# Row turns of the first expert slot placed one per two attention stages; an overflow loop over 128-row chunks; the first dense block's rows turned before that loop

## The chip, the cores and the metric

The kernel runs on one core of one Trainium2 chip. The metric is the device time of one execution in microseconds (us); the median of three runs of the kernel before is 809.47 us (807.54 to 810.33). PE is the matrix engine, DVE, ACT and POOL the vector, scalar and general engines, SP the engine that issues most DMAs.

## The reference

Three layers in float32, cut to what matters:

```
x = attention(q, k, v)             # 4 batches, 8 heads, 576 positions, 64 wide, window 128, slope bias
x = x.transpose(0,2,1,3).reshape(2304, 512)
logits = x @ w_gate + modality_bias[modality_id]      # 8 experts
e = argmax(logits); g = softmax(logits)[e]
y[rows of e] = g * (relu(x[rows of e] @ w1[e]) @ w2[e])   # 512 -> 1024 -> 512
out = relu(y @ w_in)**2 @ w_out                           # 512 -> 2048 -> 512
```

Which rows go to which expert is known only on the chip, so the number of work slots is too.

## The kernel before

**Attention** runs over 40 units (batch, 128-row tile, half of the heads), in software-pipelined stages k = 0 to 42. Stage k takes the row maximum of unit k on DVE (`smax`, L243, or L245 for the 64-row tail tiles), its exponentials on ACT (`sexp`, L264/L266, in two halves), the scores of unit k+1 on PE (L228/L230), the transposes of unit k-2 (L287) with their evictions on ACT (`ev`, L298), and the product with v of unit k-3 (L322). After every second unit a generator `post` copies a tile (L342), turns it back with the router's weights beside it (L351), scales it (L353, L354, L366, L367) and stores it to `xd`. `route` then finds, three tiles at a time, each row's expert and place (L395 to L438).

The program order is written out by hand: each engine executes its instructions in the order in which the source issues them. `background()` advances every open generator by one step; a stage calls it twice, before and after `pv`.

**The first slot** (512 rows of one expert among the first 1024 tokens) is prepared during attention by the generator `prefetch_first`: it reads the slot's row list, gathers four blocks of 128 rows (L637), loads the first weight chunks, and *turns* each block. `turn` transposes 128 x 512 on PE into a bank `v` (the bank that `tr` uses too), casts the two halves on ACT (L650) and subtracts on DVE (L652), which gives a high and a low float32r part. `wsplit` does the same for a weight chunk: the high part by a cast (L567; for the first three chunks on DVE, `quick`), the low part by a subtraction (L568; on POOL, but for the first chunk on DVE). From stage 40 the generator `up_first` puts the slot's first matrix products (L657) between the rest of attention.

**Expert slots.** Five slots are unrolled. Each is 96 matmuls up, 24 per 128 rows down, and a scatter of rows to `yd` (L693). The last 128 rows of slot 4 are held back (`ylast`): their part for the first 256 output rows is added by a 0/1 matrix (`hot`).

**The loop** (L963) does further slots of 512 rows where the routing needs them. In this execution it is not entered. Every engine branches over its body all the same, and then waits until all engines and DMAs are done.

**The dense layer** works on nine blocks of 256 rows. For block 0, after the loop, `yload(0)` loads two row tiles from `yd` (L995), four matmuls with `hot` give the held-back part (L657 into `v`), DVE adds it (L1008), and `turn` makes the split transposes (L645 into `x` and `m`, L650, L652). Then `up` and `down` follow for all blocks.

Of the kernel before, what the change touches and what calls it, by code (L numbers as in the profile page):

```python
# [20 lines left out]
E, FF = 8, 1024  # L21
# [27 lines left out]
def attention_moe_kernel(ctx, tc, qh, kh, v, mid, wg, mb, w1, w2, win, wout, out):  # L49
# [22 lines left out]
    def row(dt=F32):  # L72
        return take(("row", dt), 8, lambda: rowp.tile([128, DM], dt, tag="row", name="row"))

# [15 lines left out]
    e_int, o_int = x_int[:, 0, :], x_int[:, 1, :]  # L90
    n_int = ct([1, 1], "n_int", I32)
    again = ct([128, 1], "again")
    lbias = ct([128, NT, E], "lbias")
# [380 lines left out]
    def slots():  # L474
# [36 lines left out]

        left, oh, sw, mn, need = r1([MAXSLOT]), r1([MAXSLOT]), r1([2]), r1([1]), r1([1])
        n = ends[:, E - 1:E]
# [10 lines left out]
        dve.tensor_copy(cum[0:1, 0, :], need.to_broadcast([1, E]))  # L524
        dve.tensor_tensor(n_int, n, need, op=ALU.add)
        dve.scalar_tensor_tensor(oh[:, 1:], left[:, 1:], mn, siota[:, 1:], op0=ALU.is_le, op1=ALU.mult)
# [18 lines left out]
        dve.tensor_tensor(x, x, x2, op=ALU.add)  # L545
        dve.tensor_copy(x_int[:, :, 1:MAXSLOT], x[:, :, 1:])

    second = []
# [72 lines left out]

    def index(s, o):
        iv = sm.tile([128, 4], I32, tag="idx", name="idx", bufs=3)
        if s == 0:
            pool.tensor_copy(iv, t_first[:, bass.ds(o, 4)])
            gv = sm.tile([128, 4], I32, tag="idx", name="idx", bufs=3)
            pool.tensor_scalar(gv, iv, float(DUMP), None, op0=ALU.min)
        else:
            pool.tensor_copy(iv, t_int[:, bass.ds(o, 4)])
            gv = iv  # L630
        xr[s] = iv, {}, gv
# [7 lines left out]
    def turn(s, i, r, tag, n=512):  # L639
        if s not in xT:  # L640
            k = min(4, 1024 // n)
            xT[s] = [[wt("right", F32R)[:, :k * n].rearrange("p (c t) -> p c t", t=n) for _ in range(4 // k)] for _ in range(2)]
        p = bank(tag, (128, 4, 128))
# [10 lines left out]
    def passes(ps, pairs, first, last):  # L654
        n = len(pairs)
        for i, (l, r) in enumerate(pairs):
            pe.matmul(ps, l, r, start=first and i == 0, stop=last and i == n - 1)  # L657

# [89 lines left out]
    def prefetch_first():  # L748
        index(0, column(0))
        advance_load(2)  # L750
        yield
        for i in range(0, 4):
            gather(0, i)
            yield
        advance_split(1)
        advance_load(3)
        yield
        for i in range(4):
            turn(0, i, xr[0][1][i], "v")
            yield  # L760
            if i % 2:
                advance_split(2 + i // 2)
        primed.append(True)

    primed = []
    LA = 5
# [41 lines left out]
    for k in range(n + 3):  # L808
# [31 lines left out]
    wpools["left"] = ctx.enter_context(tc.tile_pool(name="wl", bufs=24))  # L840
    assert checked
    while not primed:
        background()
# [10 lines left out]
    def down_first(hs):  # L854
# [30 lines left out]
        advance_split(8 + LA)  # L885

    while not up:
        next(first, None)
        background()

    for s in range(NSLOT):
# [21 lines left out]
        if s == 2:  # L913
            p = bank("v", (128, E))
            pe.matmul(p, ones, cum[:, 0, :], start=True, stop=True)
            dve.tensor_scalar(again, p[:, 0:1], float(ROWS), None, op0=ALU.mult)
            total = nc.values_load(n_int[0:1, 0:1], min_val=NSLOT - 1, max_val=MAXSLOT)
        if s == 0:
            down_first(hs)
            continue  # L920
        for i in range(n // 128):
# [29 lines left out]
    conv_step(2 * len(MOE_CHUNKS) + 1)  # L951
    flush(0)


# [7 lines left out]
    held.append({})  # L962
    with tc.For_i(NSLOT - 1, total, 1) as si:  # L963
        e = nc.sync.value_load(e_int[0:1, bass.ds(si, 1)], min_val=0, max_val=E - 1)
        o = pool.value_load(o_int[0:1, bass.ds(si, 1)], min_val=0, max_val=E * NCH - 4)
        index("d", o)
        for i in range(4):
            gather("d", i)
            turn("d", i, xr["d"][1][i], "x")
        hs = []  # L970
        for f in range(8):
            if f % 2 == 0:
                wload("d", expert_src(e, f // 2))
                wsplit("d")
            hs.append(relu_split(ffn1("d", W["d"], f)))
        ps = [bank("t"), bank("t"), bank("v"), bank("v")]
        for f in range(8):
            if f % 2 == 0:
                wload("d", expert_src(e, 4 + f // 2))
                wsplit("d")  # L980
            for i in range(4):
                c = slice(128 * i, 128 * i + 128)
                ffn2(ps[i], hs[f][0][:, c], hs[f][1][:, c], W["d"], f, f == 0, f == 7)
        for i in range(4):
            put("d", i, ps[i])
    held.clear()

    yr = {}

    def yload(j):  # L990
        yr[j] = []
        for i in range(2):
            r = row()
            a = row_of(2 * j + i)
            nc.sync.dma_start(out=r, in_=yd[a:a + 128, :])  # L995
            yr[j].append(r)

    order = token_tiles()
    NB = NT // 2


    yload(0)
    s, i, y, yhl, hot = ylast
    dve.tensor_tensor(yhl[:, 512:], y, yhl[:, :512].bitcast(F32), op=ALU.subtract)
    yadd = [bank("v") for _ in range(2)]
    for j in range(2):
        passes(yadd[j], [(hot[:, 128 * j:128 * j + 128], yhl[:, 512 * k:512 * k + 512]) for k in range(2)], True, True)
        dve.tensor_tensor(yr[0][j], yr[0][j], yadd[j], op=ALU.add)  # L1008
    scatter(s, i, y)
    del ylast, y, yhl, hot, yadd, xr[s]  # L1010
    for i in range(2):
        turn(("c", 0), i, yr[0][i], "xm"[i], 256)
    flush(0)
# [156 lines left out]
```

## Time and profile before

| what | us |
|---|---|
| median of three runs | 809.47 |
| the profiled execution's own time | 807.53 |
| its span, first to last instruction | 805.8 |
| PE busy in the span | 780.5 (97%) |
| DVE, ACT, POOL busy | 407.2, 330.9, 232.9 |
| attention until the first slot's products start | 0 to 147.3 |
| five expert slots (with the end of attention) | 147.3 to 375.1 |
| from the last slot product to the first dense product | 375.1 to 385.5 |
| dense layer | 385.5 to 801.9 |

Times are us from the span's start unless a row says ns. A timeline row gives start, duration, engine, line, operation, output and input tiles, and in brackets how long the engine stood idle before it and what ended that.

### The profile page before, as it was taken

The numbers are of one execution on the slowest core, as the hardware profiler recorded it, in microseconds if no ns is written. First come the engines' busy times: TensorE is split into PE (matmuls) and PEld (weight loads), VectorE is DVE, ScalarE is ACT, GpSimd is POOL, SyncE is SP. The second block draws the span as 40 slices with busy tenths as digits, with TensorE's granted clock in tenths as the row PEclk, the third lists the DMA queues.
The fourth block names the chain that finished last, engine by engine and source line by source line (L and its number), as shares of the span: only waits on it lengthen the run. The fifth ranks groups of instructions, "written<-read, shape, count | busy, mean of one in ns | idle before, by whom it ended". The sixth has DMA issues, their size and how long they took to land.

```text
span 805.8 us, 13572 instructions
## 1 busy us (share of the span) xinstructions
PE 780.5 (97%) x4979; PEld 669.2 (83%) x4979; DVE 407.2 (51%) x1134; ACT 330.9 (41%) x890; POOL 232.9 (29%) x302
## 2 busy tenths in 40 slices
PE   6999989999999999997999999999999999999998
PEld 5877767777888888895988989898998989898896
DVE  5888788879996668695464522031212213021220
ACT  7787767335454444462543414031231404132230
POOL 3010032134544434423343505032230504122140
PEclk9999999999999999999899999999999999999999
DMA  8456360149746566351110210010101001010000
GB/s 274 158 179 192 119 197 27 67 141 357 251 165 205 187 208 209 132 197 55 40 53 27 80 53 27 1 53 1 53 1 31 22 1 53 1 53 1 27 1 27
DMA packets 39190, 79.10 MB, mean 98 GB/s; under 512 B 6608, under 2 KB 15056, under 8 KB 39120
## 3 DMA queue, kind: packets, MB, share of 16 engines
q1 hardware_dynamic: 36080, 68.23, 25.5%
q0 software_dynamic: 3040, 9.96, 3.4%
q8 instruction: 41, 0.67, 0.3%
q14 instruction: 29, 0.24, 0.1%
HBM read 62.19 MB, written 15.99 MB: 97 GB/s over the span
## 4 chain that ended last, share of the span: by engine, by line
PE 52%; DMA 0%; ACT 0%; DVE 0%; issue 0%; SPq 0%; DVEq 0%
PE t L657 20%; PE v L657 16%; PE s L657 13%; PE x L657 1%; PE m L657 1%; PE x L645 1%; PE m L645 0%; DMA row<-yd 0%; ACT w L567 0%; DVE row L1046 0%; ACT w L650 0%; DVE w L568 0%; DVE w L652 0%; DVE row L1031 0%; ACT row L1030 0%
## 5 line engine op out<-in xcount | busy, mean ns | idle before, releaser
L657 PE MATMUL t<-w,h 128*128 128x512 f32 x888 | 214.4, 397 | 0.0
L657 PEld LDWEIGHTS t<-w,h 128*128 128x128 f32 x888 | 164.4, 188 | 37.8
L1021 POOL TENSOR_TENSOR h<-row,h 128x256 fp32r<-128x256 f32 x144 | 109.5, 764 | 272.1 <-ACT h L1020 266.7
L657 PE MATMUL s<-w 128*128 128x256 f32 (+2 forms) x1176 | 181.4, 310 | 1.1 <-ACT w L650 0.7
L657 PEld LDWEIGHTS s<-w 128*128 128x128 f32 x1176 | 162.9, 191 | 12.3 <-ACT w L650 1.1
L657 PE MATMUL v<-w,h 128*128 128x512 f32 x432 | 104.7, 396 | 0.0
L657 PEld LDWEIGHTS v<-w,h 128*128 128x128 f32 x432 | 80.2, 188 | 18.7
L264 ACT ACTIVATE e<-x,m 128x256 f32<-128x256 f32 (+1 forms) x128 | 60.6, 476 | 27.8 <-DVE m L243 27.6
L568 DVE TENSOR_TENSOR w<-w 128x1024 fp32r<-128x1024 f32 x42 | 57.5, 1373 | 18.8 <-ACT w L567 18.4
L1031 DVE SCALAR_TENSOR_TENSOR row<-s,row 128x256 f32<-128x256 f32 x74 | 31.3, 423 | 70.5 <-ACT row L1030 70.3
L1020 ACT CAST h<-row 128x256 fp32r<-128x256 f32 x144 | 57.7, 400 | 5.0 <-DVE row L1031 5.0
L652 DVE TENSOR_TENSOR w<-x,w 128x512 fp32r<-128x512 f32 (+1 forms) x13 | 7.7, 605 | 90.4 <-ACT w L650 90.4
L1030 ACT ACTIVATE row<-s 128x256 f32<-128x256 f32 x74 | 28.3, 384 | 55.6 <-PE s L657 54.7
L567 ACT CAST w<-w 128x1024 fp32r<-128x1024 f32 x46 | 48.0, 1048 | 6.6 <-PE s L657 2.6
L657 PE MATMUL t<-w 128*128 128x256 f32 x384 | 48.3, 282 | 0.0
L603 POOL TENSOR_TENSOR w<-w,row 128x512 int32<-128x512 int32 x18 | 26.9, 1492 | 72.8 <-DVE row L602 41.2
L657 PEld LDWEIGHTS t<-w 128*128 128x128 f32 x384 | 47.2, 190 | 0.3
L650 ACT CAST w<-x 128x512 fp32r<-128x512 f32 (+1 forms) x13 | 6.6, 521 | 98.3 <-PE x L645 96.5
L228 PE MATMUL s<-kS,qS 64*128 64x256 f32 (+1 forms) x128 | 35.8, 406 | 5.4 <-DMA qS<-qh 5.2
L657 PE MATMUL v<-w 128*128 128x256 f32 x288 | 36.2, 282 | 0.0
L228 PE MATMUL t<-kS,qS 64*128 64x256 f32 (+1 forms) x128 | 35.9, 407 | 0.0
L657 PEld LDWEIGHTS v<-w 128*128 128x128 f32 x288 | 35.4, 190 | 0.3
(242 smaller groups left out, 1064.7 us busy)
## 6 DMA issues: line engine op xcount, KB each, us to landing
w<-w SPq DMA_DIRECT2D x40, 512.0 KB, 4.3
w<-win SPq DMA_DIRECT2D x16, 512.0 KB, 5.3
w<-wout SPq DMA_DIRECT2D x16, 512.0 KB, 3.9
xd<-row SPq DMA_DIRECT2D x22, 256.0 KB, 2.1
qS<-qh SPq DMA_DIRECT2D x19, 256.0 KB, 4.4
row<-yd SPq DMA_DIRECT2D x18, 256.0 KB, 2.6
vS<-vh SPq DMA_DIRECT2D x16, 256.0 KB, 4.1
out_dram<-row SPq DMA_DIRECT2D x16, 256.0 KB, 2.0
```

What stands on the lines that cost most here:

```text
L228: pe.matmul(s[j][:, i, c0:], qS[b, t][r, hp, :], kS[b][r, hp, 128 * t - 128 + c0:128 * t + 128], start=True, stop=True)
L264: act.activation(e[:, i, j, c0:], x[:, i, j, c0:], AF.Exp, bias=m[:, i, j:j + 1], scale=-1.0, accum_out=rinv[b, t][:, h:h + 1])
L567: (dve.tensor_copy if quick else act.copy)(h, r)
L568: (eng or dve).tensor_tensor(l, r, h.bitcast(F32), op=ALU.subtract)
L603: pool.tensor_tensor(a, a, r, op=ALU.add)
L645: pe.transpose(p[:, c, :], r[:, 128 * c:128 * c + 128], ident)
L652: dve.tensor_tensor(xl[j][:, :, o], p[:, k * j:k * j + k, :], xh[j][:, :, o].bitcast(F32), op=ALU.subtract)
L657: pe.matmul(ps, l, r, start=first and i == 0, stop=last and i == n - 1)
L1020: act.copy(g[:, 0:256], gt)
L1021: pool.tensor_tensor(g[:, 256:512], gt, g[:, 0:256].bitcast(F32), op=ALU.subtract)
L1030: act.activation(r, p, AF.Relu)
L1031: dve.scalar_tensor_tensor(gt, p, 0.0, r, op0=ALU.max, op1=ALU.mult)
```

## The change

Four edits. (1) `prefetch_first` turns its four row blocks at the second `background()` of stages 33, 35, 37 and 39 (a flag `tail` tells it the stage), where before it took one step at each call from stage 32 on; the low part of the first weight chunk is made on POOL. (2) The loop's body works on one chunk of 128 rows in place of four; its bounds and its tables (`loop_int`) count chunks. (3) The loads of the first dense block's rows are issued after the slot's second tile is scattered; `turn_first` turns these rows by float32 matmuls with the identity before the loop (and again at the end of its body), into banks kept open. (4) After the loop eight float32r matmuls add the held-back rows into the same banks, already turned; the splits are read from there.

```
@@ prefetch_first
-        advance_load(2)
+        advance_load(1)
         yield
         for i in range(0, 4):
             gather(0, i)
             yield
+        advance_load(2)
+        yield
+        advance_load(3)
         advance_split(1)
-        advance_load(3)
-        yield
         for i in range(4):
+            yield
+            while not tail[0] or (attending and i and tail[0] < at + 2):
+                yield
+            at = tail[0]
             turn(0, i, xr[0][1][i], "v")
-            yield
             if i % 2:
+                yield
                 advance_split(2 + i // 2)
@@ advance_split
-            wsplit(key, None, pool if s == 0 and j > 0 else None, chunk_sides(s, j), s == 0 and j < 3)
+            wsplit(key, None, pool if s == 0 else None, chunk_sides(s, j), s == 0 and j < 3)
@@ a stage of attention
         if k >= 3:
             pv(units[k - 3])
+        tail[0] = k
         background()
+        tail[0] = 0
@@ before the loop
+    def turn_first():
+        for c in range(4):
+            for i in range(2):
+                pe.matmul(x0[c // 2][:, c % 2, 128 * i:128 * i + 128], yr[0][i][:, 128 * c:128 * c + 128], ident, start=c % 2 + i == 0, stop=False, skip_group_check=True)
...
                 put(s, i, ps)
+                if not nxt and i == n // 128 - 2:
+                    yload(0)
...
                 act.copy(yhl[:, :512], ps)
-                dve.tensor_copy(y, ps)
+                dve.tensor_tensor(yhl[:, 512:], ps, yhl[:, :512].bitcast(F32), op=ALU.subtract)
+                act.copy(y, ps)
...
+    x0 = [bank(k_, (128, 2, 256)) for k_ in "xm"]
+    turn_first()
@@ the loop
-    with tc.For_i(NSLOT - 1, total, 1) as si:
+    with tc.For_i(4 * (NSLOT - 1), total, 1) as ci:
...
+        put("d", 0, ps)
+        yload(0)
+        turn_first()
@@ after the loop
-    yload(0)
-    dve.tensor_tensor(yhl[:, 512:], y, yhl[:, :512].bitcast(F32), op=ALU.subtract)
-    yadd = [bank("v") for _ in range(2)]
...
+        for k_ in range(2):
+            c = 2 * j + k_
+            passes(x0[j][:, k_, :], [(yhl[:, 512 * m + 128 * c:512 * m + 128 * c + 128], hot[:, 0:256]) for m in range(2)], False, True, skip_group_check=True)
+        act.copy(x0T[0][0][:, 2 * j:2 * j + 2, :], x0[j])
+    for j in range(2):
+        dve.tensor_tensor(x0T[1][0][:, 2 * j:2 * j + 2, :], x0[j], x0T[0][0][:, 2 * j:2 * j + 2, :].bitcast(F32), op=ALU.subtract)
```

In the changed kernel `turn`'s subtraction is L659, a chunk's cast L574, `route` starts at L396, `post`'s scaling is L354 to L368, `turn_first`'s matmul L918, the products L664, the loop L1003.

DVE, stages 32 and 33, before: a chunk's cast and subtraction, then the first turn's pair of subtractions, ahead of the next maximum (L243), and a second and third turn behind it.

```order
L430 TENSOR_SCALAR row<-iota,row 128x128 x3
L567 CAST w<-w 128x1024
L568 TENSOR_TENSOR w<-w 128x1024
L652 TENSOR_TENSOR w<-v,w 128x2x128 x2
L342 COPY row<-x 128x4x64
L243 ISA x,m<-s,bias 128x256
```

DVE, the end of stage 35 and stage 36, now: a turn's subtractions (L659) between `post`'s reciprocal and its scaling, then the next maximum.

```order
L354 TENSOR_SCALAR ri<-ri 128x8
L355 RECIPROCAL ri<-ri 128x8
L659 TENSOR_TENSOR w<-v,w 128x2x128 x2
L367 TENSOR_TENSOR row<-m,ri 128x384
L367 TENSOR_TENSOR ls<-m,ri 128x48
L367 TENSOR_TENSOR row<-x,ri 128x128
L367 TENSOR_TENSOR ls<-x,ri 128x16
L368 TENSOR_REDUCE l_all<-ls 128x8
L244 ISA x,m<-s,bias 128x256
```

Here the maximum of stage 36 stands behind the turn and the scaling; stages 37 and 39 read alike. The next rows of DVE hold the second chunk's cast, with `route` behind it:

```order
L574 CAST w<-w 128x1024
L396 TENSOR_TENSOR l_all<-l_all,lbias 128x24
L397 TENSOR_REDUCE mx_all<-l_all 128x3
L399 TENSOR_TENSOR row<-l_all,mx_all 128x24
L400 TENSOR_TENSOR row<-row,rev 128x24
L343 COPY row<-x 128x512
L244 ISA x,m<-s,bias 128x256
```

The cast, which frees POOL to subtract, stood in stage 33 before and has moved to stage 36; the third chunk's cast has moved in the same way to stage 40, right ahead of `route`'s L431.

PE around the loop, now: `turn_first` (L918) stands ahead of the branch, and only the eight sums stand behind it.

```order
L664 MATMUL t<-w,h 128x512 x72
L918 MATMUL x<-ident,row 128x128 x4
L918 MATMUL m<-ident,row 128x128 x4
L1003 COMPARE_AND_BRANCH
...
L1003 COMPARE_AND_BRANCH
L1003 UNCONDITIONAL_BRANCH
L664 MATMUL x<-row,w 128x256 x4
L664 MATMUL m<-row,w 128x256 x4
```

Eight float32 matmuls have moved from behind the branch (there as transposes) to a place ahead of it.

## Rows read from the trace of the kernel before

**Rows 1.** Stages: length, busy us (instructions) by engine, granted PE clock, DMA.

```profile
112.45:147.33 34.88, 31.16 (x277) 23.90 (x277) 28.96 (x126) 24.32 (x84) 5.21 (x3) 0.95 0.21 64
147.33:375.08 227.75, 225.93 (x1059) 184.95 (x1059) 178.62 (x329) 101.89 (x168) 90.88 (x86) 1.00 0.55 188
375.08:385.45 10.37, 3.98 (x13) 2.60 (x13) 3.48 (x6) 1.75 (x3) 1.05 (x2) 0.71 0.31 85
```

**Rows 2.** Timeline of ACT, stages 33 to 39.

```profile
117.46 0.51 ACT L264 ACTIVATE e<-x,m 128x256 f32<-128x256 f32 x1 [1.70 <-DVE m L243]
...
119.95 0.64 ACT L650 CAST w<-v 128x256 fp32r<-128x256 f32 x2
...
129.00 0.51 ACT L264 ACTIVATE e<-x,m 128x256 f32<-128x256 f32 x1 [2.36 <-DVE m L243]
...
132.51 0.51 ACT L264 ACTIVATE e<-x,m 128x256 f32<-128x256 f32 x1 [0.49 <-DVE m L243]
...
135.44 0.51 ACT L264 ACTIVATE e<-x,m 128x256 f32<-128x256 f32 x1
...
139.28 0.46 ACT L266 ACTIVATE e<-x,m 128x192 f32<-128x192 f32 x1 [0.82 <-DVE m L245]
...
142.49 0.46 ACT L266 ACTIVATE e<-x,m 128x192 f32<-128x192 f32 x1 [0.91 <-DVE m L245]
...
143.86 0.57 ACT L298 COPY pt<-v 128x512 f32<-128x512 f32 x1
```

**Rows 3.** Timeline of DVE, stages 32 to 40.

```profile
114.86 1.22 DVE L568 TENSOR_TENSOR w<-w 128x1024 fp32r<-128x1024 f32 x1
116.00 0.75 DVE L652 TENSOR_TENSOR w<-v,w 128x256 fp32r<-128x256 f32 x2
...
121.30 0.68 DVE L567 CAST w<-w 128x1024 fp32r<-128x1024 f32 x1
...
130.88 0.56 DVE L366 TENSOR_TENSOR row<-m,ri 128x384 f32<-128x384 f32 x1
...
132.05 0.41 DVE L243 CUSTOM_DVE_ANT_0 x<-s,bias 128x256 f32<-128x256 f32 x1
...
134.84 0.41 DVE L243 CUSTOM_DVE_ANT_0 x<-s,bias 128x256 f32<-128x256 f32 x1
...
143.98 0.11 DVE L425 SCALAR_TENSOR_TENSOR row<-row 128x3 f32<-128x3 f32 x1
...
146.24 0.85 DVE L430 TENSOR_SCALAR row<-iota,row 128x128 fp32r<-128x128 f32 x3
```

**Rows 4.** Timeline of PE, stage 40.

```profile
146.73 0.76 PE L434 MATMUL m<-row 128*128 128x160 f32 x3 [0.42 <-DVE row L430]
```

**Rows 5.** Timeline of DVE beside POOL's subtractions.

```profile
158.39 2.91 DVE L430 TENSOR_SCALAR row<-iota,row 128x128 fp32r<-128x128 f32 x3
...
171.50 0.99 DVE L481 TENSOR_TENSOR r<-r,thr 1x40 f32<-1x40 f32 x1
```

**Rows 6.** Timeline of POOL there.

```profile
158.48 2.48 POOL L568 TENSOR_TENSOR w<-w 128x1024 fp32r<-128x1024 f32 x1 [27.96 <-PE s L657]
...
170.02 2.39 POOL L568 TENSOR_TENSOR w<-w 128x1024 fp32r<-128x1024 f32 x1 [1.89 <-ACT w L567]
```

**Rows 7.** Timeline of PE around the loop.

```profile
380.80 2.07 PE L657 MATMUL v<-w,row 128*128 128x512 f32 x4 [5.72 <-DMA row<-yd]
...
385.45 4.98 PE L657 MATMUL s<-w 128*128 128x256 f32 x24 [0.68 <-ACT w L650]
```

**Rows 8.** Line L963, PE's branches: duration ns min/median/max, first and last start.

```profile
L963 PEldq COMPARE_BRANCH x3: 97/193/3921, 370.8 to 380.6; - x3
```

**Rows 9.** Line L693 at 370 to 372: last scatter before the loop.

```profile
L693 POOL DMA_INDIRECT yd<-row,idx x1: 970/970/970, 370.4 to 370.4; - x1
...
DMA to landing us min/median/max: 2.7/2.7/2.7
```

**Rows 10.** Line L995 at 376.7 to 379: loads of the first dense block.

```profile
DMA to landing us min/median/max: 2.9/3.3/3.7
```

More of the change, by code (lines that the diff above doesn't have):

```diff
@@ L72, in row @@
     def row(dt=F32):
-        return take(("row", dt), 8, lambda: rowp.tile([128, DM], dt, tag="row", name="row"))
+        return take(("row", dt), 6, lambda: rowp.tile([128, DM], dt, tag="row", name="row"))
     def bank(tag, shape=(128, 512)):
@@ L91, in attention_moe_kernel @@
     n_int = ct([1, 1], "n_int", I32)
+    loop_int = ct([1, 2, MAXSLOT, 4], "loop_int", I32)
     again = ct([128, 1], "again")
@@ L509, in slots @@
         yield
-        left, oh, sw, mn, need = r1([MAXSLOT]), r1([MAXSLOT]), r1([2]), r1([1]), r1([1])
+        left, oh, sw, mn, need, last = r1([MAXSLOT]), r1([MAXSLOT]), r1([2]), r1([1]), r1([1]), r1([1])
         n = ends[:, E - 1:E]
@@ L524, in slots @@
         dve.tensor_copy(cum[0:1, 0, :], need.to_broadcast([1, E]))
-        dve.tensor_tensor(n_int, n, need, op=ALU.add)
+        dve.tensor_tensor(last, n, need, op=ALU.add)
+        dve.tensor_scalar(n_int, last, 4.0, None, op0=ALU.mult)
         dve.scalar_tensor_tensor(oh[:, 1:], left[:, 1:], mn, siota[:, 1:], op0=ALU.is_le, op1=ALU.mult)
@@ L546, in slots @@
         dve.tensor_copy(x_int[:, :, 1:MAXSLOT], x[:, :, 1:])
+        yield
+        four = [1, MAXSLOT, 4]
+        dve.tensor_copy(loop_int[:, 0], x[:, 0, :, None].to_broadcast(four))
+        dve.tensor_tensor(loop_int[:, 1], x[:, 1, :, None].to_broadcast(four), siota[0:1, None, 0:4].to_broadcast(four), op=ALU.add)
     second = []
@@ L620, in flush, with index @@
             pend.pop(0)()
-    def index(s, o):
-        iv = sm.tile([128, 4], I32, tag="idx", name="idx", bufs=3)
+    def index(s, o, n=4):
+        iv = sm.tile([128, 4], I32, tag="idx", name="idx", bufs=3)[:, :n]
         if s == 0:
@@ L628, in index @@
         else:
-            pool.tensor_copy(iv, t_int[:, bass.ds(o, 4)])
+            pool.tensor_copy(iv, t_int[:, bass.ds(o, n)])
             gv = iv
@@ L652, in turn, with passes @@
             dve.tensor_tensor(xl[j][:, :, o], p[:, k * j:k * j + k, :], xh[j][:, :, o].bitcast(F32), op=ALU.subtract)
-    def passes(ps, pairs, first, last):
+    def passes(ps, pairs, first, last, **kw):
         n = len(pairs)
         for i, (l, r) in enumerate(pairs):
-            pe.matmul(ps, l, r, start=first and i == 0, stop=last and i == n - 1)
+            pe.matmul(ps, l, r, start=first and i == 0, stop=last and i == n - 1, **kw)
     def up_pairs(s, w, f):
@@ L841, in attention_moe_kernel @@
     assert checked
+    attending.clear()
+    tail[0] = n
     while not primed:
@@ L885, in down_first, with yload @@
         advance_split(8 + LA)
+    yr = {}
+    def yload(j):
+        if j not in yr:
+            yr[j] = [row() for _ in range(2)]
+        for i in range(2):
+            a = row_of(2 * j + i)
+            nc.sync.dma_start(out=yr[j][i], in_=yd[a:a + 128, :])
+    def turn_first():
+        for c in range(4):
+            for i in range(2):
+                pe.matmul(x0[c // 2][:, c % 2, 128 * i:128 * i + 128], yr[0][i][:, 128 * c:128 * c + 128], ident, start=c % 2 + i == 0, stop=False, skip_group_check=True)
     while not up:
@@ L962, in attention_moe_kernel @@
     held.append({})
-    with tc.For_i(NSLOT - 1, total, 1) as si:
[L964 to L969, printed above, removed]
+    le, lo = (loop_int[:, i].rearrange("p a b -> p (a b)") for i in range(2))
+    with tc.For_i(4 * (NSLOT - 1), total, 1) as ci:
+        e = nc.sync.value_load(le[0:1, bass.ds(ci, 1)], min_val=0, max_val=E - 1)
+        o = pool.value_load(lo[0:1, bass.ds(ci, 1)], min_val=0, max_val=E * NCH - 1)
+        index("d", o, 1)
+        gather("d", 0)
+        turn("d", 0, xr["d"][1][0], "s", 128)
         hs = []
@@ L974, in attention_moe_kernel @@
                 wsplit("d")
-            hs.append(relu_split(ffn1("d", W["d"], f)))
-        ps = [bank("t"), bank("t"), bank("v"), bank("v")]
+            hs.append(relu_split(ffn1("d", W["d"], f, 128), 128))
+        ps = bank("t")
         for f in range(8):
@@ L980, in attention_moe_kernel @@
                 wsplit("d")
[L981 to L985, printed above, removed]
-    held.clear()
[L988 to L996, printed above, removed]
+            ffn2(ps, *hs[f], W["d"], f, f == 0, f == 7)
+        put("d", 0, ps)
+        yload(0)
+        turn_first()
+    held.clear()
     order = token_tiles()
     NB = NT // 2
-    yload(0)
     s, i, y, yhl, hot = ylast
-    dve.tensor_tensor(yhl[:, 512:], y, yhl[:, :512].bitcast(F32), op=ALU.subtract)
-    yadd = [bank("v") for _ in range(2)]
+    xT["c", 0] = x0T = [[wt("right", F32R).rearrange("p (c t) -> p c t", t=256)] for _ in range(2)]
     for j in range(2):
-        passes(yadd[j], [(hot[:, 128 * j:128 * j + 128], yhl[:, 512 * k:512 * k + 512]) for k in range(2)], True, True)
-        dve.tensor_tensor(yr[0][j], yr[0][j], yadd[j], op=ALU.add)
+        for k_ in range(2):
[4 more added lines that the diff above has]
+        dve.tensor_tensor(x0T[1][0][:, 2 * j:2 * j + 2, :], x0[j], x0T[0][0][:, 2 * j:2 * j + 2, :].bitcast(F32), op=ALU.subtract)
     scatter(s, i, y)
-    del ylast, y, yhl, hot, yadd, xr[s]
-    for i in range(2):
-        turn(("c", 0), i, yr[0][i], "xm"[i], 256)
+    del ylast, y, yhl, hot, x0, xr[s]
     flush(0)
```

6 lines of the change are left out of this document (4 added, 2 removed).

## The prediction

> **What bounds the kernel now.** I read the windows by stage first. From the first slot product to the last, PE is busy 225.93 of 227.75 us [rows 1], and the dense layer behind it is a second unbroken run of products, from 385.5 to 801.9 us in the table. Neither has slack to give back, so whatever comes later at 147.33 or at 375.08 ends the kernel that much later. The change touches two places where PE is not full: the end of attention (31.16 of 34.88 us) and the stretch around the loop (3.98 of 10.37) [rows 1].
>
> In the first of these the timelines of ACT and DVE show which wait ends last. ACT's first exponential of a stage waits for the row maximum on DVE, by 1.70 and 2.36 us where turns and casts stand ahead of it, by 0.49 in the stage after, and not at all at 135.44 [rows 2]. So the stages with a turn are bound by DVE, and those without by ACT: one such runs from 132.51 to 135.44, 2.93 us. At the end PE waits 0.42 us for `route`'s one-hot rows (L430 on DVE, from 146.24) [rows 3, 4]; the products follow at 147.33.
>
> Around the loop the chain is different. PE's longest branch takes 3.92 us [rows 8], and PE stands idle for 5.72 us until its first product behind the loop; the rows from `yd` are given as what ended that [rows 7]. The branch and those loads (2.9 to 3.7 us [rows 10]) ran side by side, so one hid the other.
>
> **Edit 1: the turns spread over attention.** I walk from exponential to exponential on ACT, since each waits for DVE or for ACT itself.
>
> Stage 33 begins earlier. Out of DVE's way go a chunk's subtraction (1.22, now POOL's) and the pair that belongs to turn 0 (0.75 as the row gives it) [rows 3]: 117.46 - 1.22 - 0.75 = 115.49.
>
> Now the chain closes: exponentials on ACT, the turn's cast on ACT, its subtraction on DVE, and the next maximum behind that. Stage 33: from its first exponential to the turn's cast 2.49 (117.46 to 119.95), from the cast to the DVE operation behind the subtraction 1.35 (119.95 to 121.30), from a maximum to its exponential 0.46 (132.05 to 132.51) [rows 2, 3]. That is 4.30, so stage 34 begins at 119.79. It has no turn: 2.93, to 122.72. Before, the same exponential began at 129.00 [rows 2], so the change is ahead by 6.28 us here.
>
> Stage 35 has turn 1, and the order shows its subtractions ahead of `post`'s scaling and the maximum: 2.93 of ACT, then 1.35, then scaling to maximum 1.17 (130.88 to 132.05 [rows 3]), then 0.46, together 5.91. Stage 36 begins at 128.63, still 3.88 ahead of 132.51 [rows 2].
>
> Stage 36 now holds the second chunk's cast (0.68 at L567 [rows 3]) with `route` right behind it, and the cast releases POOL's subtraction. Beside such a subtraction (2.48 on POOL [rows 6]) DVE's L430 took 2.91 [rows 5], where it takes 0.85 alone [rows 3]: 2.06 lost. A second row agrees: a subtraction of 40 elements took 0.99 us and ended with POOL's second, at 172.4 to 172.5 [rows 5, 6]. By the Trainium skill ("SBUF — State Buffer", section "Who interferes with whom"), a VectorE instruction with two inputs from SBUF, or one in a fast copy mode, shuts GpSimd out of SBUF, and the reverse, while a reduction does not; those two rows agree with that, and by the rule `route`'s L399 and L431, with inputs from SBUF, would stall here too. I take 2.06. Stage 36 is DVE's 2.79 from maximum to maximum (132.05 to 134.84 [rows 3]) + 0.68 + 2.06 = 5.53, so stage 37 begins at 134.16, 1.28 ahead.
>
> Stage 37 (turn 2): 5.91 again, to 140.07; before, stage 38 began at 139.28, so the lead is spent. Stage 38 as before, 3.21 (139.28 to 142.49 [rows 2]), to 143.28. Stage 39 has turn 3 and then the third chunk's cast ahead of `route`'s L431 and L430: ACT's exponentials and eviction 1.94 (142.49 to 143.86, and 0.57 [rows 2]), 1.35, `route` 2.26 (143.98 to 146.24 [rows 3]), the cast 0.68, and 2.06 beside POOL: 8.29, where it was 3.75. L430 then begins at 151.57 instead of 146.24: **+5.3**.
>
> Bounds: if the two stalls beside POOL don't come, 4.1 less. Above, what I left out: PE arriving half a microsecond late at two turns (+1.0), and a lower granted clock where PE now waits longer; the stretch shows 0.95 on average [rows 1], and a repeat of the lost 5% of 34.88 is +1.7.
>
> **Edits 2 to 4: around the loop.** The loop is not entered, so its smaller body can change only the branch. Moved are two loads (SP), eight products ahead of the loop, and behind it the additions and two casts; the chain must be walked from the loads. They are issued after a scatter that started at 370.4 and landed 2.7 us later, at 373.1 [rows 9], and they read the tensor that it writes; I let them wait for it. A load takes 3.3 [rows 10]: 376.4. PE is out of work at 375.08 [rows 1] and waits 1.3 us; the products of `turn_first` are next in its order.
>
> These are 8 products in float32 of 128 columns. In columns they are 8 x 128 = 1,024, and the four of 512 that no longer stand behind the loop (2,048 columns) took 2.07 [rows 7]; no row shows this form. If float32 with the identity costs what those products did per column, it is 1.04; if a small moving side is no cheaper than a large one, 8 x 0.52 = 4.1 is the far end. I take 2.0, since each of these carries its own load of weights, and the clock here is 0.71 of the full one on average [rows 1]. PE is done at 378.4.
>
> Now the branch, which before began as PE's products ended at 375.1 and was covered by the loads, stands behind them. From PE's last work to its first product behind the loop it was 5.72 [rows 7]; 3.92 of that is the branch [rows 8], and the rest waits for the other engines at the loop's end. I keep 5.72: 384.1. Eight sums over 256 columns are as many columns as the four of 512 that were there, 2.07 [rows 7], to 386.2, and the last cast, as wide as an eviction of 512 (0.57 [rows 2]), to 386.8. The dense layer began at 385.45 [rows 7]: **+1.3**. What the change saves behind the loop (transposes and an addition) is spent on having loads and branch in series. If the branch stays hidden or becomes short, the result is 3.8 less; if the far end holds for the products, 2.1 more.
>
> **The sum.** 5.3 + 1.3 = +6.6. The profiled execution took 807.53 us (table), 1.94 below the median 809.47, and is inside the runs' spread. On the median's basis: 809.47 + 6.6 = 816.1 us.
>
> **The rivals.**
> *B, no stall beside POOL.* The operations behind the two casts are short and may slip past POOL's subtraction; L481's 0.99 for 40 elements speaks against it [rows 5]. 816.1 - 4.1 = 812.0.
>
> *C, the branch is short now.* The body shrinks to one chunk, so the way over it is shorter, and PE's 3.92 us might go to the 193 ns of its other branches [rows 8]: -3.7, 812.4. Against it: the same rows show only that branches differ, not that length decides. The Trainium skill ("Runtime: NRT & Kernel Launch", section "Instruction fetch mechanics") says that a taken branch to code outside the fetched window waits for a fetch; in that view a shorter body could bring the target into the window. It names no time for it; 3.92 us against 193 ns agrees with a fetch.
>
> *D, the other side: the turns hide in attention and the kernel is faster.* If stages 35 to 39 take what they took before (146.24 - 129.00 = 17.24 us to L430), since turn and scaling find idle time in ACT-bound stages, then L430 comes at 122.72 + 17.24 + 1.36 for the two casts = 141.3, a gain of 4.9, and with the loop's +1.3 the time is 805.9. ACT's idle 0.49, 0.82 and 0.91 [rows 2] speak against it: DVE is already the later one there. It decides as soon as the added cost of stages 35 to 39 stays below 6.28 - 1.3 = 5.0 us; I count 11.6.
>
> *E, more of the bounds come true.* PE late, half clock after waits, costly float32 products: up to 1.0 + 1.7 + 2.1 more, 820.9.
>
> **Chances.** About 2.4 us (0.3%) is what a measurement of this kernel can tell from no change: faster means below 807.0, slower above 811.9. Forecast 0.46, B 0.13, C 0.15, D 0.15, E 0.11. B and C together end near 808.3 and D is faster, so faster gets 0.17, same 0.17 (parts of B and C, where several terms are smaller), slower 0.66. The likeliest case's own range is 813 to 819; the range for 8 in 10 runs from 807.5, where B and C join, to 820.5.
>
> **What would show it.** Right: DVE idle ahead of the turns' subtractions (L659) in stages 35, 37 and 39, and ACT's exponential of the next stage late by that; L399 and L431 some 2 us long beside POOL's subtractions; the first slot product near 152.7 instead of 147.33; PE's long branch (L1003) again near 3.9 us, starting only after `turn_first`; first dense product 10 to 13 us after the last slot product. Wrong: a first slot product before 147 (then the walk fails at stage 35), a long branch that is gone, or loads that land before PE is out of slot work.

## The result, and the profile after

The changed kernel took 820.38 us (median of 4 runs, 819.94 to 822.76) beside 809.1 for the kernel before: ratio 1.0146, 95% interval 1.012 to 1.0173. In a second comparison on another chip it was 818.37 beside 807.01: 1.0153 (1.0134 to 1.0171). So it is slower by 11.3 to 12.4 us. The direction was forecast; the size was 6.6. The time lies at the upper end of the range of 807.5 to 820.5, and on the prediction's own basis of 809.47 the ratio gives 821.3, which is above it.

The windows of the changed kernel, by the same events as [rows 1] (attention from stage 32's first exponential, slots, the stretch around the loop, dense layer), and two stretches at half the clock. Columns: length, busy us of PE, PEld, DVE, ACT, POOL, then PE clock, DMA.

```profile
114.84:157.73 42.89, 32.26 (x265) 24.66 (x265) 31.30 (x125) 24.31 (x84) 7.06 (x3) 0.91 0.16 55
157.73:389.16 231.43, 229.34 (x1059) 187.67 (x1058) 179.35 (x332) 102.08 (x168) 91.10 (x86) 0.99 0.55 186
389.16:396.04 6.88, 3.72 (x25) 3.11 (x24) 0.71 (x2) 1.76 (x3) 1.06 (x2) 0.95 0.25 94
396.05:814.28 418.23, 417.93 (x2657) 377.03 (x2656) 109.91 (x214) 120.40 (x322) 117.34 (x150) 1.00 0.09 28
142.80:146.22 3.42, 3.42 (x24) 3.02 (x24) 1.60 (x8) 1.91 (x6) 0.00 (x0) 0.50 0.20 77
153.04:163.28 10.24, 8.21 (x36) 6.75 (x34) 7.38 (x22) 0.00 (x0) 2.34 (x1) 0.50 0.26 91
```

The kernel before, profiled again on the chip of the second comparison, for its slots and dense layer:

```profile
147.18:374.72 227.54, 225.91 (x1059) 185.12 (x1059) 178.90 (x329) 102.05 (x168) 90.90 (x86) 1.00 0.53 188
385.07:801.69 416.62, 416.31 (x2656) 376.05 (x2656) 109.17 (x213) 119.77 (x321) 117.13 (x150) 0.99 0.08 28
```

Read length by length, there are three losses that matter, one small one and one gain. With the second profile of each kernel (same chip; spans 816.8 and 805.6), the first slot product comes at 156.69 instead of 147.18 (+9.5), the slots take 230.74 instead of 227.54 (+3.2), the stretch around the loop 6.88 instead of 10.35 (-3.5), the dense layer 418.16 instead of 416.62 (+1.5), and what follows the last product 4.30 instead of 3.92 (+0.4). The sum is the spans' difference, 11.2.

Attention first. ACT's first exponentials of stages 33, 36, 37, 38 and 39 (a row: start, duration, engine, line, operation, and in brackets the idle time and what ended it), answering [rows 2]:

```profile
117.92 0.51 ACT L265 ACTIVATE e<-x,m 128x256 f32<-128x256 f32 x1 [0.48 <-DVE m L244]
...
131.56 0.51 ACT L265 ACTIVATE e<-x,m 128x256 f32<-128x256 f32 x1 [2.32 <-DVE m L244]
...
136.83 0.51 ACT L265 ACTIVATE e<-x,m 128x256 f32<-128x256 f32 x1 [2.25 <-DVE m L244]
...
142.66 0.46 ACT L267 ACTIVATE e<-x,m 128x192 f32<-128x192 f32 x1 [2.26 <-DVE m L246]
...
147.59 0.46 ACT L267 ACTIVATE e<-x,m 128x192 f32<-128x192 f32 x1 [2.02 <-DVE m L246]
```

Stages 36 to 39 now all begin with a wait of 2.0 to 2.3 us for the maximum, where before that wait was 0.91 at most. The DVE rows in front of those maxima, answering [rows 3, 5]:

```profile
129.27 0.76 DVE L659 TENSOR_TENSOR w<-v,w 128x256 fp32r<-128x256 f32 x2 [3.62 <-ACT w L657]
...
133.57 2.06 DVE L399 TENSOR_TENSOR row<-l_all,mx_all 128x24 f32<-128x24 f32 x1
...
140.43 0.76 DVE L659 TENSOR_TENSOR w<-v,w 128x256 fp32r<-128x256 f32 x2 [1.37 <-ACT w L657]
...
150.91 0.76 DVE L659 TENSOR_TENSOR w<-v,w 128x256 fp32r<-128x256 f32 x2 [1.74 <-ACT w L657]
...
154.48 2.90 DVE L431 TENSOR_SCALAR row<-iota,row 128x128 fp32r<-128x128 f32 x3
```

The idle 3.62, 1.37 and 1.74 us are DVE waiting in order for a turn's cast. L399, 24 columns wide, takes 2.06 us beside POOL's subtraction (133.24, 2.35 us), and L431 2.90 where it takes 0.85 alone.

PE in the same stretch, and around the loop (answering [rows 4, 7]):

```profile
141.91 0.25 PE L408 MATMUL m<-row,upper 128*128 128x24 f32 x1 [2.54 <-DVE ls L367]
...
142.91 1.91 PE L288 MATMUL v<-ident,e 128*128 128x128 f32 x8
...
146.47 1.09 PE L288 MATMUL v<-ident,e 128*128 128x128 f32 x8
...
157.18 0.75 PE L435 MATMUL m<-row 128*128 128x160 f32 x2 [1.74 <-DVE row L431]
157.73 1.99 PE L664 MATMUL s<-w 128*128 128x512 f32 x4
...
390.05 1.56 PE L918 MATMUL x<-ident,row 128*128 128x128 f32 x8 [0.88 <-SPq L1003]
391.44 1.06 PE L918 MATMUL m<-ident,row 128*128 128x128 f32 x8
394.64 0.73 PE L664 MATMUL x<-row,w 128*128 128x256 f32 x4 [2.14 <-issue]
395.21 0.90 PE L664 MATMUL m<-row,w 128*128 128x256 f32 x4
396.05 4.53 PE L664 MATMUL s<-w 128*128 128x256 f32 x24
```

Eight products L288 take 1.91 us at half the clock and 1.09 at the full one. The first slot product falls into a half-clock stretch that lasts to 163.28: 5.55 us at half the clock, an estimated 2.8 lost. At the loop PE waits 0.88 for the loads (issued at 387.31, landed 2.7 later), and from the end of `turn_first` to the sums 2.14, not 5.72. The branch row, answering [rows 8]:

```profile
L1003 PEldq COMPARE_BRANCH  x3: 101/187/310, 390.8 to 394.4; - x3
```

The longest branch is now 310 ns.

### The profile page after: what moved, and what is told of

Its sections match the earlier page's. It is cut to its first block, busy times and chain, and to the rows that moved or that the text cites. A ratio compares the mean times of both kernels' runs of the same rounds, so it can differ in the third digit from the quotient of the medians.

```text
span 818.6 us, 13589 instructions
## 1 busy us (share of the span) xinstructions
PE 788.4 (96%) x4991; PEld 675.7 (83%) x4991; DVE 408.3 (50%) x1133; ACT 331.9 (41%) x891; POOL 235.8 (29%) x303
## 4 chain that ended last, share of the span: by engine, by line
PE 51%; DVE 0%; issue 0%; ACT 0%; POOL 0%; POOLq 0%; DVEq 0%
PE t L664 19%; PE v L664 15%; PE s L664 13%; PE m L664 1%; PE x L664 1%; PE m L652 0%; PE x L652 0%; DVE w L575 0%; ACT w L574 0%; DVE row L1074 0%; DVE row L1059 0%; ACT row L1058 0%; DVE w L659 0%; ACT h L1048 0%; POOL spacer L699 0%
## 5 line engine op out<-in xcount | busy, mean ns | idle before, releaser
L664 PE MATMUL t<-w,h 128*128 128x512 f32 x888 | 215.2, 398 | 0.0
L664 PEld LDWEIGHTS t<-w,h 128*128 128x128 f32 x888 | 165.1, 188 | 38.0
L664 PE MATMUL s<-w 128*128 128x256 f32 (+2 forms) x1176 | 183.5, 311 | 0.5 <-DVE row L1059 0.3
L664 PEld LDWEIGHTS s<-w 128*128 128x128 f32 x1176 | 164.0, 191 | 11.9 <-DVE h L689 0.6
L664 PE MATMUL v<-w,h 128*128 128x512 f32 x432 | 105.1, 398 | 0.0
L664 PEld LDWEIGHTS v<-w,h 128*128 128x128 f32 x432 | 80.5, 188 | 18.8
L659 DVE TENSOR_TENSOR w<-x,w 128x512 fp32r<-128x512 f32 (+1 forms) x12 | 7.0, 597 | 89.7 <-ACT w L657 89.7
L574 ACT CAST w<-w 128x1024 fp32r<-128x1024 f32 x46 | 48.0, 1048 | 6.3 <-PE s L664 2.7
L664 PE MATMUL t<-w 128*128 128x256 f32 x384 | 48.6, 282 | 0.0
L664 PEld LDWEIGHTS t<-w 128*128 128x128 f32 x384 | 47.4, 190 | 0.4
L664 PE MATMUL v<-w 128*128 128x256 f32 x288 | 36.5, 282 | 0.0
L664 PEld LDWEIGHTS v<-w 128*128 128x128 f32 x288 | 35.6, 190 | 0.3
L575 POOL TENSOR_TENSOR w<-w 128x1024 fp32r<-128x1024 f32 x8 | 19.0, 2374 | 57.6 <-issue 19.1
```

Source lines behind the costliest of these rows:

```text
L574: (dve.tensor_copy if quick else act.copy)(h, r)
L575: (eng or dve).tensor_tensor(l, r, h.bitcast(F32), op=ALU.subtract)
```

## The experiments

Each ratio is to the kernel before, run on the same chip. Only `body_only` and `rows_ahead` had the changed kernel timed beside them; for the other runs the second comparison, 1.0153, stands for it, from another chip. Profiles of different kernels come from different chips too.

**One half of the change at a time.** `turns_only` is the kernel before with edit 1, `loop_only` the changed kernel with attention as before.

> The kernel before with edit 1 alone: turns at stages 33, 35, 37, 39 and the first chunk's low part on POOL; loop and dense layer as before. Theory 1 (attention lost more than forecast: the first slot product at 157.7 instead of 147.3, and some 3 us more after it at half the granted clock; the loop gave 3.5 back): 11.3 + 3.5 = about 15 slower than before, 823 to 825 us, first slot product at 156 to 158. Theory 2 (the attention part cost what was forecast, 5.3 to 6.4, and the rest came from a late start and a slower stream of products that belong to the whole program): 815 to 817, first slot product near 153.

Measured: 1.0117 (1.0086 to 1.0148), 815.8 us; first slot product at 156.18. The place is that of theory 1, the time that of theory 2: 9.4 us slower, not 15. The profiled one of the five executions took 820.33 us, the other four 815.3 to 816.2, so its stretches show more than the timed loss. Some of the loss that theory 1 put into attention must belong to the rest of the program.

> The changed kernel with attention as before: edits 2 to 4 alone. Theory 1: PE's branch takes 0.3 us where it took 3.9, and the way from the last slot product to the first dense product is 6.9 us where it was 10.4: 3.5 faster, 805 to 806. As forecast (loads and branch in series): 1.3 slower, 810.4. Theory 2 (the dense layer's products run 1.7 us slower in the changed program whatever attention does): 807 to 808.

Measured: 1.0008 (0.9994 to 1.0021), as theory 2 gave. The stretch around the loop is 6.80 us and the branch 310 ns, as theory 1 said, and the time doesn't show it. The dense layer took 417.08 us with no half clock in it, where `turns_only` took 414.62, also with none. So something in the loop's edits slows products far from the loop. (`loop_only` also holds an edit of the changed kernel that the list of four leaves out: a ring of six row buffers where before it was eight. Its first slot product comes at 147.88, so that edit does not make attention's loss.)

**The branch.** `body_only` is before with edit 2, `rows_ahead` before with edits 3 and 4 and the old body.

> Before with edit 2 alone: the loop's body for one chunk of 128 rows, its tables and bounds; rows of the first dense block loaded and turned behind the loop as before. If the length of the body decides the branch: PE's longest branch there takes 0.2 to 0.5 us where it took 3.9. The first product behind the loop still waits for the loads, which are issued after SP's own branch: no gain, within 1 us of before. Rival (the branch is long for another reason): 3 to 4 us again.

> Before with edits 3 and 4 alone: loads and turn_first ahead of the loop, sums behind it, and the old body of four blocks (with the loads and turn_first at its end). If the old body makes the branch long: 3.3 to 3.9 us, now in series behind turn_first, and 10 to 10.5 us from the last slot product to the first dense product, as before: 0 to 1.3 slower than before. If the place of the branch decides: 0.3 us, and as fast as edits 2 to 4 together.

```diff
@@ rows_ahead: the loop of before, rows loaded and turned ahead of it
-    with tc.For_i(4 * (NSLOT - 1), total, 1) as ci:
+    with tc.For_i(NSLOT - 1, total, 1) as si:
```

Longest PE branch of `body_only`, then of `rows_ahead`:

```profile
L972 PEldq COMPARE_BRANCH  x3: 97/187/310, 373.5 to 379.7; - x3
```

```profile
L992 PEldq COMPARE_BRANCH  x3: 97/193/3321, 378.4 to 385.0; - x3
```

The body decides: short body 310 ns in either place, old body 3,321 ns even behind `turn_first`. The stretch around the loop was 8.52 us with the short body alone (1.8 less than before; I had expected nothing, since the loads would hide it) and 10.23 with the rows ahead alone: loads, `turn_first` and a long branch in series, as the prediction described, and no gain. Both kernels were slower than before all the same, 1.0043 (1.0028 to 1.0059) and 1.0071 (1.0044 to 1.0098). Both hold the table `loop_int`.

**Where tiles lie.** The table takes 384 bytes per partition and moves every tile behind it by as much.

> The kernel before with one more constant of 96 int32 per partition that nothing uses: no instruction differs, but every tile placed after it lies 384 bytes further on, as the table loop_int puts them in the changed kernel. Theory 3 (the products' stream depends on where its operands lie in the on-chip memory: all five profiles with the table show 417 to 419 us for the dense layer, the three without it 414.6 to 416.6): dense layer at 418 to 419, slots at 228.1 to 228.4, 2 to 4 us slower than before, ratio 1.003 to 1.005. Rival (the instructions or where they lie decide, not the data): as before, ratio 1.000, dense layer 416.5.

```diff
     n_int = ct([1, 1], "n_int", I32)
+    unused = ct([1, 96], "unused", I32)
```

Measured: 1.0047 (1.003 to 1.0065), dense layer 418.40, slots 228.98, without one instruction changed. Its stage 32 began 2.5 us later too (114.78), which the next run doesn't show (112.18).

> The kernel before with 384 unused bytes ahead of the pool that holds the later weights, so that these tiles alone (slot weights after attention, dense weights) lie 384 bytes further on and attention's tiles, the rows and the constants lie as before. If the products' stream depends on the weights' place: dense layer 418 to 418.5 where before takes 416.5, first slot product as before, 2 to 2.5 us slower, ratio 1.002 to 1.003. If it is the rows' or constants' place, or attention's: 1.000.

```diff
+    ctx.enter_context(tc.tile_pool(name="gap", bufs=1)).tile([128, 96], F32, name="gap")
     wpools["left"] = ctx.enter_context(tc.tile_pool(name="wl", bufs=24))
```

Measured: 1.0044 (1.0025 to 1.0062). Its slots and dense layer, to be read against the second profile of before above:

```profile
147.05:375.29 228.24, 226.70 (x1059) 185.59 (x1059) 179.14 (x329) 102.02 (x168) 90.79 (x86) 1.00 0.54 188
385.62:804.09 418.47, 418.18 (x2656) 377.53 (x2656) 109.23 (x213) 119.73 (x321) 117.14 (x150) 1.00 0.08 28
```

The first slot product is where it was. The same 1,059 and 2,656 products take 0.70 and 1.85 us more, and PE is as full as before: each product is a little longer.

The dense layer's whole length mixes this with the clock. The half-clock stretch around the loop reaches into its first 24 products, by 4.2 us in the first profile of before:

```profile
379.43:389.67 10.24, 8.20 (x32) 6.82 (x33) 3.18 (x5) 1.55 (x3) 0.97 (x1) 0.50 0.30 100
```

In all profiles these 24 take from 2.98 us (`turns_only`, full clock) to 5.34. From the 25th dense product on every profile has the full clock. That stretch in the second profile of before, `pad_weights`, `loop_only` and `loop_aligned` (the last has a padded table, see below):

```profile
390.04:801.68 411.64, 411.34 (x2634) 371.08 (x2632) 108.07 (x211) 119.39 (x320) 117.13 (x150) 1.00 0.08 27
390.25:804.10 413.85, 413.57 (x2634) 372.91 (x2632) 108.12 (x211) 119.35 (x320) 117.14 (x150) 1.00 0.08 27
385.95:799.82 413.87, 413.57 (x2634) 372.90 (x2632) 108.04 (x211) 119.31 (x320) 117.34 (x150) 1.00 0.08 27
388.32:799.96 411.64, 411.35 (x2634) 370.97 (x2632) 108.16 (x211) 119.46 (x320) 117.38 (x150) 1.00 0.09 27
```

The six profiles without the shift (the two of before, `turns_only` and the three with a padded table) all take 411.6 here, on several chips. Of the eleven with it ten take 413.8 to 413.9, and `body_only` 414.5, which stays unexplained. Shown: the place of the weight tiles costs 2.2 us in the dense layer at the full clock, not 1.85. Why 384 bytes do it is not shown.

> Edits 2 to 4 with attention as before, and the table loop_int made 2,048 bytes long (only its first 384 are used), so that the tiles behind it lie as before modulo 2,048 bytes. Theory 3: the gain of 3.5 around the loop is no longer eaten by the slower stream: dense layer 414.5, slots 227.6, 803 to 804.5 us where before takes 807. Rival: as edits 2 to 4 were, within 1 us of before.

> The changed kernel with the table padded in the same way and nothing else. Theory 3: 2.5 to 3.5 us faster than the changed kernel (818.4 on a chip where before takes 807.0), ratio to before 1.011 to 1.012. Rival: 1.015 again.

```diff
-    loop_int = ct([1, 2, MAXSLOT, 4], "loop_int", I32)
+    loop_int = ct([1, 512], "loop_int", I32)[:, 0:96].rearrange("p (a b c) -> p a b c", a=2, b=MAXSLOT)
```

`loop_aligned`: 0.9968 (0.9953 to 0.9983), **0.3% faster than before**, 805.75 beside 807.85. `after_aligned`: 1.009 (1.006 to 1.012), a little under what theory 3 gave, with a wide spread (815.4 to 821.0). Loop, then dense layer of `loop_aligned`:

```profile
376.85:383.60 6.75, 3.54 (x26) 2.96 (x25) 0.71 (x2) 1.81 (x4) 1.06 (x2) 1.00 0.24 89
383.60:799.96 416.36, 416.07 (x2656) 375.50 (x2656) 109.85 (x214) 120.28 (x322) 117.38 (x150) 1.00 0.09 28
```

The dense layer looks hardly shorter than the 417.08 of `loop_only`, because it has 3.4 us at half the clock (384.43 to 387.84) and `loop_only` none: its first 24 products take 4.72 instead of 3.22, and the rest 411.64 instead of 413.87.

**Attention.** First what stands beside POOL, then the clock, then the order on DVE.

> The changed kernel with the low parts of the first three chunks on DVE (1.22 us each) instead of POOL. If DVE's operations really stall some 2 us beside POOL's subtraction at two places that PE waits for (L399 in stage 36, L431 in stage 40): 2 x (2.06 - 1.22) saved and 1.22 added in stage 33, together about 0.5 faster than the changed kernel, 819 to 821, and L399 and L431 short (0.2 and 0.85). If the stalls lie beside other waits and cost nothing: the three subtractions add up to 3.6, 823 to 824.

```diff
-            wsplit(key, None, pool if s == 0 else None, ...
+            wsplit(key, None, pool if s == 0 and j > 2 else None, ...
```

Measured: 1.0104 (1.0072 to 1.0136), some 4 us under 1.0153. The same two operations of `low_dve`:

```profile
133.67 0.18 DVE L399 TENSOR_TENSOR row<-l_all,mx_all 128x24 f32<-128x24 f32 x1
...
153.85 0.85 DVE L431 TENSOR_SCALAR row<-iota,row 128x128 fp32r<-128x128 f32 x3
```

Both stalls are gone with POOL's subtraction, so the mechanism holds. The Trainium skill ("SBUF — State Buffer", section "Who interferes with whom") says that a VectorE instruction with two inputs from SBUF, or in a fast mode, and one on GpSimd lock each other out of a shared pair of ports for a whole instruction; 2.06 and 2.90 against 0.18 and 0.85 us agree. The timed gain is more than the 0.5 expected. From stage 36 on, stages took 4.65, 5.82, 4.54 and 9.65 us (to the first slot product), where the second profile of the changed kernel shows 5.27, 6.90, 4.98 and 10.14, but its first 5.83 in stage 37. From stage 32, where the first low part adds 1.26, to the first slot product it is 42.64 beside 42.89 and 44.01 in the two profiles of the changed kernel: 0.2 to 1.4 less, about as expected. The slots take 0.8 to 1.5 less with less half clock in them; where the rest of the 4 comes from is open.

> The changed kernel with 28 products of the identity with itself into a free bank, put where PE waits: 12 behind the turn in stage 37, 4 behind that in stage 39, 12 ahead of route's product in stage 40. Nothing reads them. Theory 1 (the granted clock falls to half at 142.8 and 153.0 after PE's waits, and 3.4 and 10.2 us at half cost some 4 to 5 us): the clock stays at full from 140 to 165, the first slot product comes 1 to 2 us earlier and the slots run 2 to 3 us faster: 815 to 817. Rival (the half clock falls on waits, or falls whatever PE does): 820 to 822, and half clock in the same places.

```diff
+        if attending and tail[0] >= 38:
+            keep_busy(12)
...
+    def keep_busy(m):
+        p = bank("t")
+        for _ in range(m):
+            pe.matmul(p[:, 0:128], ident, ident, start=True, stop=True)
...
             turn(0, i, xr[0][1][i], "v")
+            if attending and i > 1:
+                keep_busy(12 if i == 2 else 4)
```

Measured: 1.0111 (1.008 to 1.0142), 3.4 us under 1.0153. Attention from stage 32 and the slots of `pe_busy`:

```profile
115.06:156.21 41.15, 36.58 (x333) 29.41 (x333) 31.16 (x125) 24.42 (x84) 7.56 (x4) 1.00 0.18 65
156.21:384.79 228.58, 226.63 (x1059) 185.55 (x1059) 179.57 (x332) 101.99 (x168) 91.09 (x86) 1.00 0.54 189
```

The granted clock is full in both, stage 38 takes 3.31 us where it took 4.93, and the slots take 2.85 less than in the first profile of the changed kernel (2.2 less than in the second). From stage 33 to the first slot product it is 38.07 us beside 39.81 and 40.93. Products that nobody reads made the kernel faster: where they fill PE's waits the clock does not fall. (The two timed intervals overlap a little, the spans are 814.1 against 818.6 and 816.8.)

> The changed kernel with prefetch_first stepped last in background(): in stages 35, 37 and 39 post's scaling stands ahead of the turn's subtractions on DVE, and a chunk's cast behind route's first step; nothing else moves. If the in-order DVE queue is what a turn costs: the scaling (1.17 us) is done while DVE waits for the turn's cast, so stages 35 and 37 last 5.2 and 4.7 us instead of 6.4 and 5.8, and the time is 2 to 3.5 us under the changed kernel's, ratio 1.011 to 1.013. If ACT's cast and the next maximum decide whatever stands between: 1.015.

```diff
+        todo.sort(key=lambda g: g.gi_code.co_name == "prefetch_first")
         todo = [g for g in todo if next(g, True) is None]
```

Measured: 1.0038 (1.0024 to 1.0051), far better than expected; but the sort moved the casts too, so the next run moves the order alone.

> The changed kernel with the turn's subtractions behind post's scaling on DVE in stages 35, 37 and 39, and the casts of the second and third chunk where the changed kernel has them (the kernel with the turn stepped last moved those too, behind route's L397 and L431, and took ratio 1.0038). If the scaling's order makes the gain: ratio 1.004 to 1.006 here too. If the third cast's place (its subtraction on POOL beside L431) makes most of it: 1.010 to 1.013, L431 still 2.9 us long and the first slot product 2 us later than with the turn stepped last.

```diff
+        go = sorted(todo, key=lambda g: g.gi_code.co_name == "prefetch_first") if tail[0] else todo
+        alive = [g for g in go if next(g, True) is None]
+        todo = [g for g in todo if g in alive]
```

Measured: 1.0076 (1.0048 to 1.0104), between the two expectations. The first slot product comes at 150.62 instead of 156.69. Counted from stage 33 it is 34.93 us instead of 40.93: stage 35 1.16 shorter (the scaling, as expected), stage 37 1.10, stage 38 2.19, stage 39 with the rest 1.55. Stage 37 is 5.79 and not the expected 4.7; it was 5.83 in the first profile of the changed kernel, so nothing of it is shown to be the scaling. In that stretch the granted clock stays full:

```profile
112.61:150.62 38.01, 30.39 (x277) 23.13 (x277) 31.34 (x125) 24.30 (x84) 7.55 (x4) 1.00 0.20 70
```

It falls to half for 3.4 us right behind, from 150.90, and the slots take 229.84. Beside `pe_busy`, which is at the full clock too (38.07), the order on DVE is worth about 3.1 us in itself; the clock that it saves is the other 2.9 in the second profile of the changed kernel and 1.7 in the first. L431 is still 2.90 long here and 0.85 with the turn stepped last, where the third cast stands behind it (2.6 us less from stage 33 to the first slot product). Order and stall are both real.

> The changed kernel with three repairs: turn stepped last, the table padded to 2,048 bytes, and the second chunk's low part on DVE (1.22 us in stage 36 in place of a stall of 2.06). From the stages of the kernel with the turn stepped last (35.4 us from stage 32 to the first slot product, before 34.9) less 0.8: as long as before; with the loop's 3.5 and the dense layer as before: 3 to 4 faster than before, ratio 0.995 to 0.997, level with the kernel that has the loop's edits alone and the padded table (0.9968). If the half clock comes back somewhere: 0.998 to 1.000.

Measured: 0.9986 (0.9968 to 1.0003), 804.44 beside 805.85, not the 0.995 to 0.997 expected; the three repairs bring the spread turns back to the time before, and nothing shows a gain over edits 2 to 4 alone with the padded table (0.9968). Its stages, slots and dense layer:

```profile
113.14:147.68 34.54, 30.24 (x276) 23.13 (x277) 27.95 (x125) 24.29 (x84) 2.86 (x2) 1.00 0.22 77
147.68:376.01 228.33, 226.27 (x1059) 184.90 (x1059) 180.73 (x333) 101.95 (x168) 93.64 (x87) 1.00 0.55 189
382.86:797.70 414.84, 414.56 (x2656) 374.00 (x2656) 109.83 (x214) 120.27 (x322) 117.23 (x150) 1.00 0.09 28
```

In the profile, which has no half clock up to 800.85, it is 3.6 under before (span 802.0 against 805.6). The timed runs show 1.1 to 1.4, and their interval includes no difference.

**The two kernels once more.**

> The kernel before once more, for a profile on the same chip as the experiments. If the dense layer's slower stream (1.7 us more from first to last product in the changed kernel's first profile) belongs to the chip and the run: some 414.5 us from the first to the last dense product here too, and nothing of it is due to the change. If it belongs to the program: 416.1 as in the first profile of before.

> The changed kernel once more, timed beside before on one chip. From the steps of the profiles that come back (first slot product some 8 late, slots some 3 longer by half clock, loop 3.5 shorter): ratio 1.009 to 1.010, 7 to 8 us. If the first comparison holds as it stands: 1.0146, 11 to 12 us, and then something that the steps don't show is in it.

Before took 416.62 in the dense layer, as in its first profile (416.48), and the changed kernel 1.0153: the "7 to 8" counted from the profiles was wrong because I had written the slower dense layer off as a matter of the chip. These two runs sent me to the addresses.

## Why the prediction was right in direction and wrong in size

**Start of stage 33: right.** Forecast 115.49; 115.76 in the second profile of the changed kernel and 115.29 in `turns_only`. In its first profile it was 117.92: 0.83 from the first loads on, and one wait of DVE (L367, 2.18 us where before and the second profile have 0.63). That wait is unexplained, and nothing rests on it.

**The walk through the stages: 0.9 short at full clock, 2.6 to 3.8 short with the clock's part.** Stages 33 to 38 and the rest to the first slot product, forecast: 4.30, 2.93, 5.91, 5.53, 5.91, 3.21, 9.38 (8.29 and 1.09 from L430 to the product). First profile: 4.30, 2.93, 6.41, 5.27, 5.83, 4.93, 10.14. Second: the same but 6.90 in stage 37 and 4.98 in stage 38. The forecast is 37.17 together, `pe_busy` at the full clock 38.07, the two profiles 39.81 and 40.93. Stage 35 lacks the half microsecond by which PE came late, which I left out by name; stage 38 lacks 1.7, nearly all of which `pe_busy` gives back (3.31). The failing step is "Above, what I left out": the clock was put at 1.7 for attention, outside the sum, where the runs show 1.7 to 2.9, and nothing was put for what comes after it. The half clock reaches 5.55 us into the slots (4.61 in the second profile), where every microsecond is PE's: an estimated 2.3 to 2.8 more.

**The two stalls beside POOL: right.** The forecast was 2.06 lost at each; L431 lost 2.05 (2.90 instead of 0.85) and L399 1.88 (2.06 instead of 0.18). Rival B falls by these rows, and `low_dve` shows the cause.

**The loop: wrong; rival C happened.** "I keep 5.72" failed. The wait for the loads (0.88, forecast 1.3) and `turn_first` (2.45 from 390.05, forecast 2.0) came as described, and then 2.14 instead of 5.72: 0.31 of branch and 1.83 of the rest, which I had at 3.92 and 1.80. `body_only` and `rows_ahead` show that the body's length decides. That fits the sentence on taken branches in the Trainium skill ("Runtime: NRT & Kernel Launch", section "Instruction fetch mechanics"); no run here shows the fetch itself. The sums were over in 1.4, not 2.6 with the cast; the 2.07 of the four products that priced them was taken inside the half-clock stretch of before (379.43 to 389.67). Together -3.5 where +1.3 stood: 4.8 too much.

**What was not in the sum at all.** "The loop is not entered, so its smaller body can change only the branch" failed too. The prediction gives no term for the table `loop_int`; it is 384 bytes ahead of the weights, and those cost 0.70 in the slots and 2.2 in the dense layer (`pad_weights`, 1.0044 timed). The changed kernel's dense layer is only 1.5 longer because less half clock falls into its first 24 products: 4.30 us in its second profile, 4.97 in that of before.

**Rival D** (faster) fell at its own point: from the start of stage 35 to L431 it is 29.33 us (125.15 to 154.48), 12.1 more than the 17.24 to L430 before, not under 5. So that 6.6 comes as near to 11.3 as it does is luck: two errors partly cancel, 4.8 too much at the loop and some 9 too little elsewhere. Of the 9, by the second profiles, some 4.5 are the clock (2.9 in attention, an estimated 2.3 in the slots, 0.7 back in the dense layer), 2.9 the addresses, and the rest the walk, the start and what follows the last product.

What stays open: why two profiles of one kernel place the half-clock stretches differently (142.8 and 153.0 in the first, two between 134 and 144 and one at 154 in the second), why the shift of the weights slows the products, and what the 0.4 us behind the last product are.

## What to carry to other kernels

Work that is spread over an in-order queue costs where it waits, not what it computes: put what is ready (here the scaling) ahead of what must be waited for. When waits in front of a matrix engine that is otherwise full grow, count the half clock behind them as well, and past the end of the stage. And before a new constant is priced by its instructions, look at which tiles it moves; padding it so that the others keep their place modulo a power of two, here 2,048 bytes, is a cheap test.

## What the runs showed of the hardware

- 384 unused bytes ahead of the weight tiles lengthened the dense layer from its 25th product on from 411.64 to 413.85 us at the same count of products and the full clock, and padding the shift to 2,048 bytes took it back (411.64 in `loop_aligned`).
- PE's branch over a loop that is not entered took 310 ns over a short body and 3.3 to 3.9 us over a long one.
- Eight products on PE took 1.91 us at half the granted clock and 1.09 at the full one; 28 products without use kept the clock full from 115 to 385 us and saved more than they cost (1.0111 instead of 1.0153).
- Beside a subtraction of 2.35 us on POOL an operation of 24 columns on DVE took 2.06 us, and 0.18 without it.
